# Pooled attention and channel mixing on one core: whole-head preparation and position mixing by a difference

## The chip, the cores and the metric

One NeuronCore of a Trainium2 chip runs the whole program. The metric is the device time of one execution in microseconds, the median over runs. PE, DVE, ACT, POOL and SP are the core's engines: TensorE (matrix products), VectorE, ScalarE, GpSimd and SyncE, the queue that issues the DMAs here.

## What is computed

q, k and v have 8 batches, 8 heads, 1152 positions and 64 channels. Queries are averaged in pairs (576 rows), attention runs over 1152 keys, and the result, with the heads side by side (512 channels), goes through a gated channel mixing:

```python
q_pool = q.reshape(B, H, S // 2, 2, D).mean(axis=3)
scores = scale * np.matmul(q_pool, k.transpose(0, 1, 3, 2))
attn = np.exp(scores - np.max(scores, axis=-1, keepdims=True))
attn = attn / (np.sum(attn, axis=-1, keepdims=True) + 1e-09)
x = np.matmul(attn, v)                        # then heads side by side: (8, 576, 512)
x_prev = np.concatenate([zeros, x[:, :-1, :]], axis=1)
xk = mu_k * x + (1.0 - mu_k) * x_prev
xr = mu_r * x + (1.0 - mu_r) * x_prev
kk = np.maximum(xk @ w_k, 0.0)                # w_k 512 x 1024
vv = kk * kk @ w_v                            # w_v 1024 x 512
out = vv / (1.0 + np.exp(-(xr @ w_r)))        # w_r 512 x 512
```

## The kernel before, in words

**Precision.** Every factor of a product is a pair of 16-bit numbers, a high half and the low half that is left, and a product is the sum of three (high-high, high-low, low-high). So each prepared operand takes a rounding to its high half (ACT), a subtraction that gives the low half (POOL or DVE), and both are stored.

**Attention.** The 64 heads (`n`) of 576 pooled queries are cut into 6 blocks of 96 queries (`NB`, `QN`): 384 blocks. `block` makes the scores of a block into one of three PSUM tiles `s` in two passes of nine products (L528 with the high half of Q, L533 with the low half). Between them DVE takes the maximum over the nine key chunks (L550), PE turns it with the identity (L553), DVE takes the small maximum (L561), and ACT writes it as a row into the Q operand (L542), so that the second pass subtracts it. ACT then takes the exponential (L575) and POOL splits off its low part (L537). `window` sums P x V into the PSUM tile `a` in five windows per head (L602, L604, L607: 18 sums for the first, 27 for each other), DVE divides (L628), and two heads together are turned, from the second batch on with two transposing DMAs, into `xt`, where channels are partitions and positions columns.

**Heads ahead.** `prep` makes K and V of a head: two loads; ACT's rounding of K (L468); the low half of K on POOL (L473, on DVE for head 0); a transposing DMA and a copy; ACT's scaled rounding of V (L492); V's low half on DVE (L495); V for the low products on POOL (L498). `queries` does two heads' Q: load, pair sum (L423, DVE), rounding (L426, ACT), low half (L430, DVE), two transposing DMAs. Both work in two parts, chunks 0 to 4 and 5 to 8.

**Weights.** `weights` brings w_k (8 pieces), w_r (4) and w_v (8): a load, two ACT conversions (L687, L691), a merge on DVE (L694), ACT's rounding (L704), the low half on POOL (L709). The first 8 pieces go by the tiles `ex`, the others by one tile `lw`.

**Channel mixing.** `ff` works on tiles of 256 positions, 18 in all. `mix` makes `xk` and `xr` by channel group (4 groups of 128): ACT scales the earlier position by 1 - mu into a tile `tmp` (L741), DVE multiplies the position by mu and adds (L744). For `xk` ACT rounds (L750); for both POOL takes the low half (L752). A tile then has 96 key products of 256 columns (`wk`), 24 gate products (`wr`) and 48 value products (`wv`) of 512 columns, all at L772. The positions of a tile may lie in two batches; then the steps are split (192 and 64, or 128 and 128).

**Order of issue.** Each step is recorded with `op(engine, duration, function, reads, writes, key)`. `Issue.run` does not sort by key: for each engine it takes the steps in an order that is stored as a compressed table of numbers, `TURNS`. The engines run their queues in that order and wait for one another only by data. `gaps` puts spare matmuls on zeros (L902) into PE's planned pauses of the first 150 us.

The key products of the last batch's tiles may use the PSUM tiles of the scores too (`f_psum`).

## Time and profile before

| | us |
|---|---|
| median of 3 runs | 1087.14 (1086.99 to 1087.65) |
| the profiled execution | 1090.2 |
| its span, first to last instruction | 1088.4 |
| PE busy | 1064.6 (98%) |
| DVE busy | 847.8 (78%) |
| ACT busy | 840.6 (77%) |
| POOL busy | 806.3 (74%) |

Busy time is the time in which at least one instruction of an engine is under way, so one that starts before its neighbour has ended adds only its rest. A matmul is under way from its issue to the end of its result. L numbers are lines of the kernel before; an instruction is named out<-in by the program's tiles.

### The profile page before, as it was taken

Reading aid. Unit: us, or ns where it says so; the run is one execution under the profiler, and the core shown is the slowest. Engines: PE = TensorE matmul, PEld = TensorE weight load, DVE = VectorE, ACT = ScalarE, POOL = GpSimd, SP = SyncE. Lnnn points to the kernel's source line nnn. Section 1 sums busy time; section 2 is a strip of 40 time slices with the busy share of each in tenths; the row PEclk is TensorE's granted clock in tenths of the full one; section 3 lists DMA queues with packets and bytes.
Section 4 is the critical chain, followed back from the end, with each engine's and each line's share of the span. In section 5 each row is a group of like instructions: output and inputs, shape, how many; then the busy total and the mean of one; then the engine's idle time right before and its main releaser. Section 6 shows DMA issues by size and latency. Waiting matters only on the chain.

```text
span 1088.4 us, 43891 instructions
## 1 busy us (share of the span) xinstructions
PE 1064.6 (98%) x18599; PEld 872.8 (80%) x18599; DVE 847.8 (78%) x1590; ACT 840.6 (77%) x1804; POOL 806.3 (74%) x940
## 2 busy tenths in 40 slices
PE   8899999999999999999999999999999999999998
PEld 7888877879698888888697979788787979787664
DVE  7999989888778888788677878787878887774321
ACT  7999987887778887787877788788778778775643
POOL 5889887876787876886777877778677877776431
PEclk9999999999999999999999999999999999999999
DMA  9997838665667664583646646666455565430001
GB/s 229 249 218 182 177 106 187 142 135 111 132 133 145 133 126 112 107 158 85 147 105 127 134 95 143 128 113 147 90 129 125 105 158 116 87 58 20 20 20 39
DMA packets 258148, 135.29 MB, mean 124 GB/s; under 512 B 193440, under 2 KB 230304, under 8 KB 257952
## 3 DMA queue, kind: packets, MB, share of 16 engines
q1 hardware_dynamic: 257952, 132.50, 56.6%
q8 instruction: 145, 2.38, 0.9%
q14 instruction: 51, 0.42, 0.1%
HBM read 67.11 MB, written 9.44 MB: 70 GB/s over the span
## 4 chain that ended last, share of the span: by engine, by line
PE 81%; DVE 5%; issue 1%; ACT 1%; DMA 0%; POOL 0%; SPq 0%; DVEq 0%; ACTq 0%; POOLq 0%
PE f L772 34%; PE s L528 11%; PE s L533 11%; PE a L602 7%; PE a L604 6%; PE a L607 5%; PE s L772 5%; PE s L553 2%; PE a L772 2%; DVE mx L550 2%; DVE vt L495 1%; DVE xr L744 0%; DMA vr<-in_v_dram 0%; DVE mx L561 0%; DVE xk L744 0%
## 5 line engine op out<-in xcount | busy, mean ns | idle before, releaser
L550 DVE TENSOR_REDUCE mx<-s 128x96 f16<-128x864 f32 x384 | 402.6, 1052 | 61.0 <-PE s L528 36.4
L537 POOL TENSOR_SCALAR pl<-pf 128x864 f16<-128x864 uint16 (+1 forms) x384 | 335.0, 872 | 132.6 <-ACT pf L575 106.4
L575 ACT ACTIVATE pf<-s 128x864 int32<-128x864 f32 x384 | 339.4, 887 | 103.3 <-PE s L533 82.6
L602 PE MATMUL a<-vt,pf 128*128 128x65 f16 x2880 | 309.3, 193 | 1.8 <-DVE xb L628 0.7
L604 PE MATMUL a<-vt,pf 128*128 128x64 f16 x2880 | 309.7, 193 | 0.0
L604 PEld LDWEIGHTS <-pf 128*128 128x128 f16 x2880 | 251.4, 98 | 19.0 <-issue 2.5
L602 PEld LDWEIGHTS <-pf 128*128 128x128 f16 x2880 | 256.9, 98 | 11.2 <-issue 0.6
L607 PE MATMUL a<-vb,pl 128*128 128x65 f16 x2304 | 257.7, 193 | 0.7 <-POOL pl L537 0.7
L528 PE MATMUL s<-qT,ks 128*128 128x96 f16 x3456 | 224.8, 206 | 4.2 <-ACT pf L575 2.7
L533 PE MATMUL s<-qT,ks 128*128 128x96 f16 x3456 | 223.8, 206 | 3.6 <-ACT qT L542 1.8
L607 PEld LDWEIGHTS <-pl 128*128 128x128 f16 x2304 | 212.6, 97 | 1.1 <-POOL pl L537 0.9
L528 PEld LDWEIGHTS <-ks 128*128 128x128 f16 x3456 | 186.1, 98 | 31.1 <-issue 5.4
L533 PEld LDWEIGHTS <-ks 128*128 128x128 f16 x3456 | 181.5, 98 | 21.9 <-issue 3.5
L561 DVE TENSOR_REDUCE mx<-s 128x1 f16<-128x128 f32 x324 | 93.3, 288 | 73.3 <-ACT qT L542 70.8
L772 PE MATMUL f<-xhk,wk_hi 128*128 128x256 f16 x496 | 135.2, 273 | 0.8 <-DVE em L836 0.6
L772 PE MATMUL f<-xlk,wk_hi 128*128 128x256 f16 x496 | 135.1, 272 | 0.4 <-POOL xlk L752 0.4
L772 PE MATMUL f<-xhk,wk_lo 128*128 128x256 f16 x496 | 135.2, 273 | 0.0
L542 ACT ACTIVATE qT<-s 1x96 f16<-1x96 f32 x384 | 90.0, 234 | 50.2 <-PE s L553 37.2
L772 PEld LDWEIGHTS <-wk_hi 128*128 128x128 f16 x1152 | 104.7, 98 | 16.3 <-issue 1.0
L473 POOL TENSOR_TENSOR kn<-kr,kn 128x256 f16<-128x256 f32 (+1 forms) x126 | 98.2, 784 | 17.7 <-ACT kn L468 11.0
L803 POOL TENSOR_TENSOR gl<-g 128x512 f16<-128x512 f32 x72 | 76.6, 1066 | 46.4 <-ACT g L801 43.8
L772 PE MATMUL f<-wv_hi,gl 128*128 128x512 f16 x240 | 91.0, 379 | 0.0
(120 smaller groups left out, 2046.2 us busy)
## 6 DMA issues: line engine op xcount, KB each, us to landing
kr<-in_k_dram SPq DMA_DIRECT2D x64, 288.0 KB, 3.7
vr<-in_v_dram SPq DMA_DIRECT2D x64, 288.0 KB, 3.3
qr<-in_q_dram SPq DMA_DIRECT2D x32, 320.0 KB, 3.9
ks<-ks SPq DMA_DIRECT2D x64, 144.0 KB, 3.3
out_dram<-em SPq DMA_DIRECT2D x36, 256.0 KB, 2.7
qr<-in_q_dram SPq DMA_DIRECT2D x32, 256.0 KB, 3.6
xt<-in_moe_w_v_dram SPq DMA_DIRECT2D x8, 512.0 KB, 4.0
st<-in_moe_w_k_dram SPq DMA_DIRECT2D x4, 512.0 KB, 6.1
```

Source lines behind the costliest of these rows:

```text
L473: lambda cs=cs, en=nc.vector if ve else nc.gpsimd: en.tensor_tensor(kn[i][:, cs, D:P], kr[i][:, cs], kn[i][:, cs, 0:D], op=ALU.subtract),
L528: nc.tensor.matmul(cols(c, c + 1), ks1[hp][:, c, :], qhi, start=(c == c0), stop=False, skip_group_check=True)
L533: nc.tensor.matmul(cols(c, c + 1), ks2[hp][:, c, :], qlo, start=False, stop=True, skip_group_check=True)
L537: op("POOL", 0.917 if buf == ("pside",) else NC * (r1 - r0) / 1200 + 0.27, lambda: nc.gpsimd.tensor_scalar(to, half(pf, U16, 0)[:, :, HALF ...
L542: op("ACT", 0.131, lambda: nc.scalar.activation(qlo[0:1], src, AF.Prelu, scale=scale, alpha=(1.0 + EPS) / (1.0 - EPS)), r=[("s", at)] + kl ...
L550: op("DVE", 0.974, lambda: nc.vector.tensor_reduce(mxz[:, P - QN:P], grid(0, NC).rearrange("p c q -> p q c"), axis=AX.X, op=ALU.max), r=[( ...
L561: op("DVE", 0.199, lambda: nc.vector.tensor_reduce(to, s[:, 0:P], axis=AX.X, op=ALU.max), r=[("s", z), ("row", z)], w=[("col", z1) if join ...
L575: op("ACT", NC * QN / 1200 + 0.067, lambda: nc.scalar.activation(pf[:, :, HALF + rows.start:HALF + rows.stop], grid(0, NC), AF.Exp, bias=S ...
L602: nc.tensor.matmul(a_b[:, a0:a0 + VN], half(pf, F16, 1)[:, c, his], vt[jv][:, c, D:D + VN], start=(w == 0 and c == 0), stop=False, skip_gr ...
L604: nc.tensor.matmul(a_b[:, a0:a0 + D], half(pf, F16, 1)[:, c, his], vt[jv][:, c, 0:D], start=False, stop=(side and c == NC - 1), skip_group ...
L607: nc.tensor.matmul(a_b[:, a0:a0 + VN], pl[:, c, rows], vb[jv][:, c, 0:VN], start=False, stop=(c == NC - 1), skip_group_check=True)
L772: nc.tensor.matmul(ps, terms[i][0], terms[i][1], start=(first and i == 0), stop=(i == last), skip_group_check=True)
```

## The change

Four things change, and the order of issue with them.

- `prep` and `queries` work on a whole head (or pair of heads) in one step from the second on; only the first keeps its two parts. The low half of K is DVE's for heads 0 to 7 (`KLO = 8`), POOL's after.
- The low half of the first 12 weight pieces (w_k and w_r) is DVE's (`WLO = 12`), and `lw` has two buffers.
- Mixing takes one difference x - x_prev per pair of channel groups (on DVE, written into the tile of `xr`), and each blend is one multiply-add of the difference with the earlier position. ACT's scaled copies and `tmp` go. The rounding of `xk` is one step per pair, its low half one step per pair on DVE; the low half of `xr` is one step per pair on POOL. The three small scalings of mu go.
- The table `TURNS` is another one (not shown).

```diff
 EARLY = 8
 JOIN = 60
+KLO, WLO = 8, 12
...
-    lw = const.tile([P, 512], F32, name="lw")
+    lw = bufs("lw", 2, [P, 512], F32)
...
         JS = ((0, 5), (5, NQ))
-        for j0, j1 in JS:
+        for j0, j1 in JS if n == 0 else ((0, NQ),):
...
-        for c0, c1 in ((0, 5), (5, NC)):
+        parts = ((0, 5), (5, NC)) if n == 0 else ((0, NC),)
+        for c0, c1 in parts:
...
-            ve = n == 0
+            ve = n < KLO
...
-                if mode == "W3":
+                if iss.nw <= WLO:
+                    op("DVE", 0.6, lambda lo=lo, e=e, hi=hi: nc.vector.tensor_tensor(lo, e, hi, op=ALU.subtract),
+                       r=[ke, ("w", n, c, f)], w=[("wl", n, c, f)], key=key, port=True)
+                elif mode == "W3":
...
-    def mix(w, t0, t1, key, dk):
...
-                op("ACT", ln / 1200 + 0.187, lambda x=x, s0=s0, ln=ln, z=z, c=c: nc.scalar.activation(
-                    tmp[z][:, 0:ln], x[:, c, s0:s0 + ln], AF.Copy, scale=o[:, c:c + 1]),
-   r=xk + [("omu", w)], w=[("tmp", z)], key=key + c * dk)
-                op("DVE", ln / 960 + 0.13, lambda x=x, s0=s0, ln=ln, o0=o0, z=z, c=c: nc.vector.scalar_tensor_tensor(
-                    xm[w][:, c, o0:o0 + ln], x[:, c, s0 + 1:s0 + 1 + ln], m[:, c:c + 1], tmp[z][:, 0:ln],
-                    op0=ALU.mult, op1=ALU.add),
-                   r=xk + [("tmp", z)], w=[("x", w, c, t > t0)], key=key + c * dk, port=True)
...
+    def blend(w, t0, t1, c, key):
+
+        for x, s0, ln, o0, g_, xk in parts(t0, t1):
+            op("DVE", ln / 960 + 0.13, lambda x=x, s0=s0, ln=ln, o0=o0: nc.vector.scalar_tensor_tensor(
+                xm[w][:, c, o0:o0 + ln], xm["r"][:, c, o0:o0 + ln], mu[w][:, c:c + 1], x[:, c, s0:s0 + ln],
+                op0=ALU.mult, op1=ALU.add),
+               r=xk(c) + [("mu", w), ("x", "r", c, g_)], w=[("x", w, c, g_)], key=key, port=True)
+
+    def mix_k(t0, t1, key, dk):
+        n = t1 - t0
+        for c0, c1 in PAIRS:
+            cs = slice(c0, c1)
+            for x, s0, ln, o0, g_, xk in parts(t0, t1):
+                op("DVE", 2 * ln / 960 + 0.069, lambda x=x, s0=s0, ln=ln, o0=o0, cs=cs: nc.vector.tensor_tensor(
+                    xm["r"][:, cs, o0:o0 + ln], x[:, cs, s0 + 1:s0 + 1 + ln], x[:, cs, s0:s0 + ln], op=ALU.subtract),
+                   r=xk(c0) + xk(c0 + 1), w=[("x", "r", c, g_) for c in range(c0, c1)], key=key, port=True)
+            for c in range(c0, c1):
+                blend("k", t0, t1, c, key)
+            op("ACT", 2 * n / 1200 + 0.083, lambda cs=cs: nc.scalar.activation(
+                xh[:, cs, 0:n], xm["k"][:, cs, 0:n], AF.Copy, scale=SK),
+               r=both("k", c0, c1), w=[("xh", c0)], key=key)
+            op("DVE", 2 * n / 960 + 0.069, lambda cs=cs: nc.vector.scalar_tensor_tensor(
+                xl["k"][:, cs, 0:n], xm["k"][:, cs, 0:n], SK, xh[:, cs, 0:n], op0=ALU.mult, op1=ALU.subtract),
+               r=both("k", c0, c1) + [("xh", c0)], w=[("xl", "k", c0)], key=key, port=True)
+            key += 2 * dk
+
+    def mix_r(t0, t1, key, dk):
+        n = t1 - t0
+        hi = top(xm["r"])
+        for c0, c1 in PAIRS:
+            cs = slice(c0, c1)
+            for c in range(c0, c1):
+                blend("r", t0, t1, c, key)
+            op("POOL", 2 * n * 0.0019 + 0.2, lambda cs=cs: nc.gpsimd.tensor_tensor(
+                xl["r"][:, cs, 0:n], xm["r"][:, cs, 0:n], hi[:, cs, 0:n], op=ALU.subtract),
+               r=both("r", c0, c1), w=[("xl", "r", c0)], key=key)
+            key += 2 * dk
```

The lines of the changed kernel are others: its large maximum is L534, the small one L545, the merge of weights L678, their low half L690, a blend L733, the difference L743, the low half of xk L751, and the projections L784.

**DVE in the first heads.** mx and mb are the outputs of the large and the small maximum of a block, ex the merge of a weight piece, vt the low half of V. Before, DVE's queue reads here:

```order
L550 TENSOR_REDUCE mx_98<-s_134 128x96
L561 TENSOR_REDUCE mb_100<-s_133 128x1
L694 SCALAR_TENSOR_TENSOR ex_120<-f,xt_107 128x512
L561 TENSOR_REDUCE mb_101<-s_134 128x1
L495 SCALAR_TENSOR_TENSOR vt_89<-vr_75,vt_89 128x4x64
L694 SCALAR_TENSOR_TENSOR ex_119<-f,st_123 128x512
L495 SCALAR_TENSOR_TENSOR vt_89<-vr_75,vt_89 128x5x64
L550 TENSOR_REDUCE mx_96<-s_132 128x96
```

With the change, at the same head:

```order
L534 TENSOR_REDUCE mx_98<-s_133 128x96
L545 TENSOR_REDUCE mb_100<-s_132 128x1
L690 TENSOR_TENSOR wk_lo<-ex_117,wk_hi 128x512
L545 TENSOR_REDUCE mb_101<-s_133 128x1
L678 SCALAR_TENSOR_TENSOR ex_118<-f,xt_107 128x512
L479 SCALAR_TENSOR_TENSOR vt_89<-vr_75,vt_89 128x9x64
L534 TENSOR_REDUCE mx_96<-s_131 128x96
```

The two halves of V have become one step, and a low half of a weight piece (wk_lo), formerly POOL's, stands between two small maxima.

**DVE where a tile is mixed, in the middle of the program.** Before (xk and xr are blends that read ACT's tmp):

```order
L744 SCALAR_TENSOR_TENSOR xk<-xt_107,mu_k,tmp_118 128x256
L744 SCALAR_TENSOR_TENSOR xk<-xt_107,mu_k,tmp_117 128x256
L827 SCALAR_TENSOR_TENSOR ex_120<-ex_120,em_122 128x512
L836 SCALAR_TENSOR_TENSOR em_122<-f,ex_120 128x512
L550 TENSOR_REDUCE mx_97<-s_133 128x96
```

With the change:

```order
L743 TENSOR_TENSOR xr<-xt_107 128x512
L733 SCALAR_TENSOR_TENSOR xk<-xr,mu_k,xt_107 128x256 x2
L545 TENSOR_REDUCE mx_97<-s_131 128x1
L411 TENSOR_TENSOR qs_78<-qr_77 128x576
L534 TENSOR_REDUCE mx_97<-s_132 128x96
L743 TENSOR_TENSOR xr<-xt_107 128x512
L751 SCALAR_TENSOR_TENSOR xlk<-xk,xhk 128x512
L545 TENSOR_REDUCE mx_98<-s_132 128x1
```

The difference (xr<-xt) comes first, both blends of the pair read it, and the low half of xk (xlk) is DVE's now.

**PE behind the last sum of attention.** wr products belong to the gate of tile 14, wk products to tile 15, wv products to the values of tile 14. Before, the key products stand ahead of the second half of the gate:

```order
L772 LDWEIGHTS wk_lo
L772 MATMUL s_134<-xhk,wk_lo 128x256
L772 LDWEIGHTS wk_hi
L772 MATMUL s_134<-xhk,wk_hi 128x256
L772 LDWEIGHTS xr
L772 MATMUL f<-wr_hi,xr 128x512
L772 LDWEIGHTS xr
L772 MATMUL f<-wr_lo,xr 128x512
```

With the change the gate's twelve products come first, then seventeen value products, and only then the first key product of tile 15:

```order
L784 MATMUL f<-wr_lo,xr 128x512
L784 LDWEIGHTS xlr
L784 MATMUL f<-wr_hi,xlr 128x512
L784 LDWEIGHTS g_113
L784 MATMUL f<-wv_hi,g_113 128x512
L784 LDWEIGHTS g_113
L784 MATMUL f<-wv_lo,g_113 128x512
```

On SP's queue the 31 later Q loads are one transfer each in place of two. PE has 26 more spare matmuls (146 for 120), all before the first products of a tile or shortly after them.

## Rows read from the trace of the kernel before

**Rows 1.** The page's first part: busy us (share of the span) and instructions.

```profile
PE 1064.6 (98%) x18599; PEld 872.8 (80%) x18599; DVE 847.8 (78%) x1590; ACT 840.6 (77%) x1804; POOL 806.3 (74%) x940
```

**Rows 2.** The chain of waits: start us, us, what (pieces of dense stretches).

```profile
165.53 1.51 PE f L772 x7
...
424.98 0.03 PE a L604
...
425.13 0.06 PE s L553
425.19 0.38 PE s L528 x9
...
426.44 0.66 PE f L772 x6
```

**Rows 3.** Busy time by stretch: start:end, its length, busy us of each engine.

```profile
10.00:105.00 95.00, 86.31 (x1940) 77.74 (x1937) 88.73 (x172) 88.10 (x189) 80.00 (x92) 1.00 0.96 221
105.00:193.00 88.00, 84.46 (x1542) 70.77 (x1539) 82.10 (x138) 76.77 (x167) 74.06 (x80) 1.00 0.69 155
193.00:980.00 787.00, 781.93 (x14194) 650.44 (x14191) 638.30 (x1194) 616.74 (x1328) 606.37 (x709) 1.00 0.58 121
980.00:1083.00 103.00, 103.00 (x849) 66.28 (x847) 30.24 (x59) 53.54 (x112) 42.39 (x51) 1.00 0.07 21
```

**Rows 4.** Groups on PE from 193 to 980 us; last, L772 alone in that stretch.

```profile
L604 PE MATMUL a<-vt,pf 128*128 128x64 f16 x2250 | 243.8, 193 | 0.0
...
L607 PE MATMUL a<-vb,pl 128*128 128x65 f16 x1800 | 202.4, 193 | 0.4 <-POOL pl L537 0.4
L528 PE MATMUL s<-qT,ks 128*128 128x96 f16 x2701 | 177.0, 206 | 0.4 <-ACT pf L575 0.3
...
L553 PE MATMUL s<-identb,mx 128*128 128x128 f16 x301 | 66.2, 220 | 2.4 <-DVE mx L550 2.2
...
193.00:980.00 787.00, 444.41 (x2192) 185.76 (x2192) 1.00 0.58 121
```

**Rows 5.** Groups from 10 to 105 us: xcount | busy us, mean ns | idle before.

```profile
L473 POOL TENSOR_TENSOR kn<-kr,kn 128x320 f16<-128x320 f32 x9 | 7.9, 882 | 0.6 <-ACT kn L468 0.2
...
L473 POOL TENSOR_TENSOR kn<-kr,kn 128x256 f16<-128x256 f32 x8 | 5.4, 680 | 0.5
...
L709 POOL TENSOR_TENSOR wk_lo<-ex,wk_hi 128x512 f16<-128x512 f32 x7 | 8.2, 1170 | 2.4 <-PE s L565 1.9
...
L694 DVE SCALAR_TENSOR_TENSOR lw<-lw,xt 128x512 int32<-128x512 int32 x5 | 4.0, 796 | 0.0
...
L495 DVE SCALAR_TENSOR_TENSOR vt<-vr,vt 128x320 f16<-128x320 f32 x7 | 3.6, 510 | 0.0
...
L495 DVE SCALAR_TENSOR_TENSOR vt<-vr,vt 128x256 f16<-128x256 f32 x7 | 3.2, 453 | 0.0
...
L694 DVE SCALAR_TENSOR_TENSOR ex<-f,xt 128x512 int32<-128x512 int32 x4 | 2.7, 679 | 0.0
```

**Rows 6.** Groups of the whole program: the mixing's blend, low half and scaled copies.

```profile
L744 DVE SCALAR_TENSOR_TENSOR xk<-xt,mu_k,tmp 128x256 f32<-128x256 f32 (+3 forms) x96 | 54.2, 571 | 12.0 <-ACT tmp L741 11.5 <-ACT qT L542 0.5
...
L752 POOL TENSOR_TENSOR xlk<-xk,xhk 128x256 f16<-128x256 f32 x72 | 50.7, 711 | 14.4 <-ACT xhk L750 12.0
...
L741 ACT ACTIVATE tmp<-xt,omu_r 128x256 f32<-128x256 f32 (+3 forms) x96 | 42.4, 445 | 9.8 <-DVE xr L744 6.1 <-DVE xk L744 3.5
```

**Rows 7.** DVE in order of time: start us, us, instruction.

```profile
975.72 1.06 DVE L550 TENSOR_REDUCE mx<-s 128x96 f16<-128x864 f32 x1
976.69 0.73 DVE L744 SCALAR_TENSOR_TENSOR xk<-xt,mu_k,tmp 128x64 f32<-128x64 f32 x2
```

**Rows 8.** Groups from 105 to 193 us: the late merges of weights.

```profile
L694 DVE SCALAR_TENSOR_TENSOR lw<-lw,xt 128x512 int32<-128x512 int32 x7 | 6.9, 988 | 0.0
```

**Rows 9.** Waits from 193 to 980 us: us in total, times, longest us.

```profile
DVE mx L561 <- ACT qT L542: 67.1, 113, 1.6
...
PE s L553 <- DVE mx L550: 2.2, 5, 0.7
```

More of the change, by code (lines that the diff above doesn't have):

```diff
@@ L594, in window @@
         VN = D + 1
-        vk = [(x, jv, c0) for x in ("vt", "vtl") for c0 in (0, 5)]
+        vk = [(x, jv, c0) for x in ("vt", "vtl") for c0 in ((0,) if n else (0, 5))]
         js = range(r0 // QN, (r0 + size - 1) // QN + 1)
@@ L683, in v_ @@
                     op("DVE", dur, fn, r=r, w=w, key=key, port=late)
-                u, kf = (lw, ("lw",)) if late else (f_b, ("f",))
+                u, kf = (lw[i], ("lw", i)) if late else (f_b, ("f",))
                 ui = u.bitcast(I32)
@@ L714 @@
     out_f = out.rearrange("b t m -> (b t) m")
-    cnt = {"r32": 0, "ex": 0, "f": 0, "tmp": 0}
+    cnt = {"r32": 0, "ex": 0, "f": 0}
     def turn(n, m=2):
@@ L743, in mix @@
[L743 to L754 removed]
+    PAIRS = [(c, c + 2) for c in range(0, NG, 2)]
@@ new lines, in parts, with both @@
+    def parts(t0, t1):
+        t = t0
+        while t < t1:
+            b = t // TQ
+            e = min(t1, (b + 1) * TQ)
+            s0, ln = t - b * TQ, e - t
+            yield xt[b % 3], s0, ln, t - t0, t > t0, lambda c, b=b, s0=s0, ln=ln: [
+                ("xt", b % 3, c, k0) for k0, k1 in TURN if spans(k0, k1)[0] < s0 + ln and spans(k0, k1)[1] > s0 - 1]
+            t = e
+    def both(w, c0, c1):
+        return [("x", w, c, g_) for c in range(c0, c1) for g_ in (False, True)]
+    def blend(w, t0, t1, c, key):
[4 more added lines that the diff above has]
+               r=xk(c) + [("mu", w), ("x", "r", c, g_)], w=[("x", w, c, g_)], key=key, port=True)
```

215 lines of the change are left out of this document (89 added, 126 removed).

## Prediction

> **What bounds the kernel now.** I first read the page's busy line [rows 1]: PE is busy 1064.6 of 1088.4 us, the other three engines 74 to 78%. That says "TensorE", but a matmul counts as busy while it waits in the pipe, so the second look is at PE's pace. In the chain of waits of a dense stretch nine score matmuls take 0.38 us, six 256-column products 0.66 us, one sum 0.03 us, one identity turn 0.06 us; seven 512-column products take 1.51 us [rows 2]. That is 0.042, 0.11, 0.03, 0.06 and 0.216 us each.
>
> [...] From 193 to 980 us PE issues 6300 sums (two of 2250 and one of 1800), twice 2701 scores, 301 turns and 2192 projection products [rows 4]. A tile has 96 products of 256 columns and 72 of 512, a mean of (96 x 0.11 + 72 x 0.216) / 168 = 0.155 us. So 189 + 228 + 18 + 341 = 776 us of work in 787 us: only some **11 us** are free there. From 980 to 1083 us PE is never idle. The start is different. From 10 to 105 us there are 48 blocks and hardly a projection: 48 x 18 scores x 0.042, at most 8 heads of 126 sums (18 + 4 x 27 in the code) x 0.03 and 48 turns make at most 70 us of work in 95. Here PE waits, and DVE (88.7 us), ACT (88.1) and POOL (80.0) are all nearly full [rows 3]. The stretch from 105 to 193 us is between: DVE 82.1 of 88.
>
> So a gain has two places: about 25 us of PE's free time in the first 105 us, where three engines are full at once, and about 11 us spread over the long middle.
>
> **First stretch (10 to 105 us).** DVE's order up to the 48th row maximum tells what comes and goes. In come seven low halves of K, each 576 columns, and eight low halves of weights of 512. DVE does not show the first at that size. Two halves of V cost 0.510 + 0.453 = 0.963 us; the slope between them (57 ns for 64 columns) gives 0.74 for a whole head [rows 5]. These are the ends; I take 0.75, since the slope comes from the same operation. The weights cost 0.68 as the merge of the same size does [rows 5]. With one difference and one low half of xk (0.68 each, by the same row) that is 7 x 0.75 + 8 x 0.68 + 1.4 = 12.1 us. Out go five late merges (x 0.80 = 4.0), which come later, two blends (1.1 [rows 6]) and fifteen second halves of Q and V, each worth 0.963 - 0.75 = 0.2 (3.0; at the other end nothing). The sum is **+4 us on DVE**, +7 if joining halves saves nothing.
>
> POOL loses seventeen half steps of K (7.9 + 5.4 us) against three whole ones, which cost 0.882 + 0.680 = 1.6 at most, eleven low halves of weights at 1.17 and two of xk at 0.71: 13.3 - 4.7 + 12.9 + 1.4 = **23 us less of 80** [rows 5, 6]. ACT loses four weight chains of three instructions, each at least the 0.445 us of a 256-column step [rows 6], hence 5 us or more, and a fixed part per joined step.
>
> What is late next is therefore DVE. Its 88.7 + 4 would leave 2 of 95 us, but its busy time counts tails that overlap: a row maximum of 1.06 us is followed by the next start after 0.97 [rows 7]. With up to 0.09 us for each of 172 instructions there is room, up to 15 us, which no row settles. With ACT and POOL out of the way I expect DVE to wait less: **-2 us**, between -8 (it closes most gaps) and +4 (every added us lands).
>
> **105 to 193 us.** DVE gets the five late merges (0.99 each in this stretch [rows 8]), four more low weights (2.7), three differences and three low halves of xk (4.1), and loses three blends (1.7), eleven second halves (2.2) and a query step (0.8): +7 on 82.1 of 88. POOL loses 3, ACT the scaled copies of the mixing. PE's own work is some 81 us, so there is little to win. I take **0**, from -3 to +5.
>
> **The middle.** Over the whole program ACT loses 192 scaled copies (2 x 42 us) and POOL 72 low halves of xk (50.7) [rows 6]. DVE keeps the 192 blends and gains a difference and a low half per pair: 48 + 36 operations of up to 0.68 us, at most 57 us. Joining halves gives back 125 x 0.2 = 25. DVE waits 67.1 us for ACT's row write before its small maximum; PE waits for the large maximum, 2.2 us, more than for anything else [rows 9]. A freer ACT shortens the first, a fuller DVE lengthens the second. As 11 us are the most there is to win, I take **-3**, from -8 to +3.
>
> The Q loads lose their halves (31 fewer transfers on SP's queue); they are issued twelve blocks ahead, so I cost the later landing at nothing, and if that cover went, the first score of every second head would wait. The 26 extra filler matmuls stand in planned pauses: 26 x 0.06 = 1.6 us of PE time, nothing unless a pause is gone.
>
> **The end.** The difference is written into the tile of xr, so no tile's key mixing can start before the products of the tile before have read xr. That is a new wait. PE's order now puts the second half of tile 14's gate products ahead of the first key product of tile 15. Behind the last read of the first column pair stand six gate and seventeen value products, 23 x 0.216 = 5.0 us. The chain to cover is a difference (0.68), two blends (2 x 0.57), a copy of 512 columns (under 0.68) and a low half (0.68): 3.2 us and four hand-overs [rows 5, 6]. I cost it at **0**, at most 2 us for each of the last three tiles if DVE is held up.
>
> **Sum.** -2 + 0 - 3 + 0 = -5 us on the profiled execution, whose own time is 1090.2 us (a span of 1088.4 and 1.8 around it). That lies 3.1 us above the median of the runs shown, 1087.14; taken off the median, it gives **1082 us**.
>
> **The rivals.**
> *DVE becomes the bound (slower).* The place is 10 to 193 us. DVE is busy 170.8 of 183 us there, and 4 + 7 are added: 181.8. If its free time cannot be pressed below the 12 us that it has now, the stretch grows by what is added, less what POOL's smaller share lets go: +7, or **1094 us**. It decides as soon as the gaps before the row maxima stay as they are. For it: merges of one size cost 0.68 at one place, 0.80 and 0.99 at others [rows 5, 8], so DVE's work swells where POOL also reads. Against it: POOL is 23 us lighter in just this stretch.
> *xr as a turnstile (slower).* If the chain above takes 7 us in place of 5, PE stands 2 us at each of the last three tiles, where it now has no pause [rows 3]: **1093 us**.
> *Hidden anyway.* DVE's load cancels what ACT and POOL give, and PE's order has the same work: 1087 us.
> *POOL was the true bound of the start.* DVE's two-input steps and POOL's steps hold one another up: the same merge at 0.68, 0.80 and 0.99 us. If they exclude one another, POOL's 80.0 us, DVE's V steps (7 x 0.963 = 6.7), late merges (4.0) and Q steps fill the 95 us, and 23 less on POOL against 8 more on DVE open it until DVE's work ends last: -9 there, -4 in the middle, **1074 us**. [...]
> That the change doesn't do what it says is no rival: the order shows each step where the text puts it.
>
> **How the numbers follow.** A measurement can tell 0.2% (2.2 us) from no change: under 1085.0 is faster, over 1089.3 slower. Chances: the forecast (1077 to 1085) 0.40; POOL as the bound (1068 to 1077) 0.14; hidden 0.18; DVE as the bound (1090 to 1099) 0.20; the turnstile (1090 to 1095) 0.08. So faster 0.54, same 0.18, slower 0.28. The range 1071 to 1095 leaves out the lower part of the POOL case and the upper part of the DVE case, some 0.14. As both signs carry weight, the likeliest case's own range is 1077 to 1085.
>
> **What would show it.** Right: the 48th row maximum starts at 103 us or sooner, DVE busy there at about 92 of 93 us, POOL under 60; PE's free time in the middle under 11 us; no PE wait for xlk after the last sum. Wrong: the 48th block later than 105 us with DVE at its full share, or gaps on PE ahead of the key products of tiles 15 to 17.

## The result, and the profile after

| | before | after |
|---|---|---|
| median of 4 runs, same chip | 1087.39 us | 1103.59 us (1100.48 to 1105.45) |
| ratio, 95% interval | 1 | 1.0139 [1.0108, 1.0170] |
| span of the profiled execution | 1088.4 us | 1098.7 us |

The change is slower by 1.4%; the forecast was 0.5% faster. The profiled execution of after is the fastest of its four, and that of before (1090.2 us) is slower than three of the four beside it, so the two spans lie only 10.3 us apart where the medians lie 16.2 apart: the traces account for 10.3 us. Run again as a control, the changed kernel gives 1.0130 and a span of 1100.6. The page's busy line of after, against [rows 1]:

```profile
PE 1068.2 (97%) x18625; PEld 875.1 (80%) x18625; DVE 873.6 (80%) x1565; ACT 763.0 (69%) x1419; POOL 746.4 (68%) x750
```

ACT lost 78 us and POOL 60, DVE gained 26 and PE 3.6; no other engine is near full, yet the span grew by 10.3. Where it grew is read from the start of the same large maximum in both traces (the blocks numbered from 0). Block 48 starts 3.8 us later than before (108.9 for 105.1), block 80 4.6, the last block 9.6, and the end comes 10.3 later: **3.8 us in the first stretch, 0.8 in the second, 5.0 in the middle, 0.7 at the end**. In the control it is 5.2, 0.2, 6.0 and 0.7. The same stretches of after by windows, to be held against [rows 3] (start:end, length, busy us of PE, weight loads, DVE, ACT and POOL, granted clock, DMA share, GB/s):

```profile
10.00:109.00 99.00, 88.41 (x1957) 80.01 (x1955) 92.47 (x168) 81.11 (x156) 59.56 (x64) 0.98 0.93 199
109.00:198.00 89.00, 85.11 (x1524) 70.57 (x1521) 82.67 (x136) 74.49 (x143) 70.11 (x64) 1.00 0.66 158
198.00:990.00 792.00, 784.11 (x14220) 652.17 (x14218) 653.49 (x1160) 558.73 (x1034) 580.54 (x582) 1.00 0.59 122
990.00:1094.00 104.00, 102.37 (x842) 65.10 (x840) 36.62 (x75) 42.17 (x76) 32.82 (x31) 1.00 0.10 21
```

In the first row POOL fell from 80.0 to 59.6 and ACT from 88.1 to 81.1, DVE rose from 88.7 to 92.5: each as forecast. But the stretch is 4 us longer, and the granted clock is 0.98 where it was 1.00. The windows inside show where, first before, then after:

```profile
20.00:24.00 4.00, 2.84 (x68) 2.54 (x66) 3.47 (x5) 3.61 (x7) 3.41 (x5) 1.00 1.36 254
24.00:28.00 4.00, 3.85 (x98) 3.69 (x99) 2.99 (x7) 3.26 (x9) 2.00 (x4) 1.00 0.83 279
28.00:32.00 4.00, 3.62 (x89) 3.29 (x85) 3.87 (x10) 4.00 (x7) 3.67 (x5) 1.00 1.20 242
```

```profile
20.00:24.00 4.00, 3.99 (x114) 3.86 (x110) 3.63 (x6) 3.84 (x7) 3.41 (x4) 1.00 0.97 311
24.00:28.00 4.00, 1.29 (x24) 1.30 (x25) 1.71 (x4) 0.99 (x2) 0.17 (x1) 0.81 1.20 157
28.00:32.00 4.00, 3.48 (x58) 3.25 (x56) 2.46 (x4) 2.88 (x6) 0.00 (x0) 0.76 1.14 177
```

From 20 to 24 us PE issues 114 matmuls where it issued 68; then it stands for most of four microseconds and the others do little, and the clock is 0.81 and 0.76 over these windows (0.50 from 26.5 to 29.9 us). PE and its weight loads by time in after (start, us, instruction, in brackets the idle time before it and what ended it):

```profile
23.76 0.19 PE L588 MATMUL a<-vt,pf 128*128 128x64 f16 x1
23.79 0.20 PE L591 MATMUL a<-vb,pl 128*128 128x65 f16 x1
...
26.70 0.10 PEld L586 LDWEIGHTS <-pf 128*128 128x128 f16 x1 [2.84 <-issue]
26.71 0.24 PE L586 MATMUL a<-vt,pf 128*128 128x65 f16 x1 [2.72 <-issue]
26.76 0.25 PE L588 MATMUL a<-vt,pf 128*128 128x64 f16 x1
26.81 0.25 PE L591 MATMUL a<-vb,pl 128*128 128x65 f16 x1
```

PE stops for 2.7 us in the middle of a window of sums whose operands are all there: "issue" means that no semaphore ended the pause. Behind it the sums stand 0.05 us apart instead of 0.03, at this clock of 0.50. Before has one such pause, of 0.6 us at 73.4 us.

The waits of the middle (195 to 1000 us: who waits for whom, us in total, times, longest), against [rows 9]:

```profile
PE s L537 <- DVE mx L534: 3.8, 10, 1.0
PE s L537 <- DVE mx L545: 1.8, 4, 0.7
```

Before, PE waited 2.2 us for the maxima; now 5.6 for both: 3.4 us more, of the middle's 5.0. So three places are to be explained: a stop without a wait, waits for DVE in the middle, and 0.7 us at the end.

### The profile page after: what moved, and what is told of

The parts are those of the page before. It is cut to its first block, busy times and chain, and to the rows that moved or that the text cites. A ratio compares the mean times of both kernels' runs of the same rounds, so it can differ in the third digit from the quotient of the medians.

```text
span 1098.7 us, 43186 instructions
## 1 busy us (share of the span) xinstructions
PE 1068.2 (97%) x18625; PEld 875.1 (80%) x18625; DVE 873.6 (80%) x1565; ACT 763.0 (69%) x1419; POOL 746.4 (68%) x750
## 3 DMA queue, kind: packets, MB, share of 16 engines
q1 hardware_dynamic: 257456, 132.49, 57.3%
q8 instruction: 145, 2.38, 0.9%
## 5 line engine op out<-in xcount | busy, mean ns | idle before, releaser
L521 POOL TENSOR_SCALAR pl<-pf 128x864 f16<-128x864 uint16 (+1 forms) x384 | 353.7, 921 | 190.5 <-ACT pf L559 157.9
L534 DVE TENSOR_REDUCE mx<-s 128x96 f16<-128x864 f32 x384 | 402.4, 1052 | 57.1 <-PE s L512 39.8
L586 PE MATMUL a<-vt,pf 128*128 128x65 f16 x2880 | 302.0, 193 | 4.2 <-issue 2.7
L588 PE MATMUL a<-vt,pf 128*128 128x64 f16 x2880 | 302.3, 193 | 0.0
L591 PE MATMUL a<-vb,pl 128*128 128x65 f16 x2304 | 254.2, 193 | 0.0
L545 DVE TENSOR_REDUCE mx<-s 128x1 f16<-128x128 f32 x324 | 92.9, 287 | 66.0 <-ACT qT L526 64.0
L784 PE MATMUL f<-xhk,wk_hi 128*128 128x256 f16 x496 | 135.1, 272 | 0.9 <-DVE em L848 0.7
L784 PE MATMUL f<-xlk,wk_hi 128*128 128x256 f16 x496 | 135.1, 272 | 0.2 <-DVE xlk L751 0.2
L784 PE MATMUL f<-xhk,wk_lo 128*128 128x256 f16 x496 | 135.2, 273 | 0.0
L784 PEld LDWEIGHTS <-wk_hi 128*128 128x128 f16 x1152 | 105.8, 98 | 15.1 <-issue 1.3
L815 POOL TENSOR_TENSOR gl<-g 128x512 f16<-128x512 f32 x72 | 79.0, 1104 | 39.7 <-ACT g L813 25.9
L537 PE MATMUL s<-identb,mx 128*128 128x128 f16 x384 | 84.5, 221 | 8.9 <-DVE mx L534 5.6
L784 PE MATMUL f<-wv_hi,g 128*128 128x512 f16 x240 | 90.9, 379 | 1.2 <-ACT ex L832 1.2
```

Of the source, the lines that this page charges most:

```text
L521: op("POOL", 0.917 if buf == ("pside",) else NC * (r1 - r0) / 1200 + 0.27, lambda: nc.gpsimd.tensor_scalar(to, half(pf, U16, 0)[:, :, HALF ...
L534: op("DVE", 0.974, lambda: nc.vector.tensor_reduce(mxz[:, P - QN:P], grid(0, NC).rearrange("p c q -> p q c"), axis=AX.X, op=ALU.max), r=[( ...
L537: op("PE", 0.057, lambda: nc.tensor.matmul(s[:, 0:P], mxz, identb, start=False, stop=False, skip_group_check=True), r=[("mx", z), ("col", ...
L545: op("DVE", 0.199, lambda: nc.vector.tensor_reduce(to, s[:, 0:P], axis=AX.X, op=ALU.max), r=[("s", z), ("row", z)], w=[("col", z1) if join ...
L586: nc.tensor.matmul(a_b[:, a0:a0 + VN], half(pf, F16, 1)[:, c, his], vt[jv][:, c, D:D + VN], start=(w == 0 and c == 0), stop=False, skip_gr ...
L588: nc.tensor.matmul(a_b[:, a0:a0 + D], half(pf, F16, 1)[:, c, his], vt[jv][:, c, 0:D], start=False, stop=(side and c == NC - 1), skip_group ...
```

## The experiments

The middle's waits are given below as in that view, the two rows of the maxima added. The expectations also count them otherwise: by how much later than the median distance PE reaches the identity turns (about 5 us before, 10 after and 11 in the control, with delays under 0.12 us left out). All ratios are to the kernel before on the same chip; stops and waits are those of one profiled execution each.

| kernel | ratio [95%] | block 48 later by | PE's stops without a wait, to 80 us | waits for maxima |
|---|---|---|---|---|
| control: after again | 1.0130 [1.0113, 1.0147] | 5.2 | 3.7 | 6.3 |
| e1 a load later | 1.0152 [1.0127, 1.0176] | 4.1 | 3.1 | 5.3 |
| e8 fillers in halves | 1.0110 [1.0090, 1.0130] | 3.2 | 2.7 | 7.3 |
| e2 difference in its own tile | 1.0135 [1.0120, 1.0150] | 3.8 | 3.7 | 6.3 |
| e3 low half of xk on POOL | 1.0242 [1.0221, 1.0263] | 5.5 | 4.6 | 8.9 |
| e14 without low half of xk | 1.0123 [1.0103, 1.0144] | 8.0 | 4.4 | 6.9 |
| e17 and without difference | 1.0104 [1.0089, 1.0118] | 4.1 | 4.7 | 6.3 |
| e15 without the second V | 1.0130 [1.0111, 1.0149] | 3.8 | 3.0 | 6.5 |
| e5 after, table 1 | 1.0077 [1.0059, 1.0095] | 5.3 | 3.9 | 2.9 |
| e9 after, table 2 | 1.0103 [1.0080, 1.0126] | 4.9 | 2.8 | 3.7 |
| e6 before, table 1 | 1.0061 [1.0041, 1.0081] | 6.3 | 0.7 | 4.5 |
| e13 before, table 2 | 0.9979 [0.9968, 0.9990] | 1.1 | 0.9 | 1.0 |
| e7 whole heads, table 1 | 1.0021 [1.0010, 1.0033] | 2.3 | 0.5 | 2.0 |
| e10 whole heads, table 2 | 1.0032 [1.0020, 1.0044] | 3.3 | 2.0 | 0.7 |
| e11 mixing, table 2 | 1.0103 [1.0087, 1.0119] | 4.6 | 4.0 | 2.3 |
| e12 both, low halves on POOL, table 2 | 1.0041 [1.0021, 1.0060] | 6.1 | 4.6 | 2.6 |
| e18 e12, fillers in halves | 1.0041 [1.0026, 1.0056] | 1.4 | 1.4 | 2.8 |
| e19 e9, fillers in halves | 1.0042 [1.0029, 1.0056] | 2.7 | 0.4 | 3.0 |

### The stop at 24 us

The control is the changed kernel with no edit.

> The changed kernel once more, nothing edited, so that its parts can be told beside the edits on the same chip. In its first trace PE stands from 23.99 to 26.71 us in the middle of a group of nine sums, at matmuls that wait for no engine, the granted clock is 0.76 to 0.81 from 24 to 32 us, and the 16th row maximum starts 4.3 us later than before. If that is a cause that belongs to the kernel, the pause is there again, 2 to 3 us at 24 us. If it was an accident of one execution, it is gone here and the time is some 4 us less than in the other runs. Either way the end should show 2.1 us of PE's waiting for xlk and the key mixing near 1010 and 1019 us, and the middle PE's waits for the large maximum of some 10 us in all.

It repeats the loss. A first guess at the stop was that PE's code, whose transfers the page counts on the same 16 DMA engines as the loads (0.9% of their span, the loads' queue 57.3%), was late behind three loads of weights in a row. e1 issues the third behind the transposition for Q (the spare matmuls, which follow from the plan, become five fewer with it):

```diff
 SP: st<-w_k, ks, xt<-w_k
-xt<-w_k
 qT<-qn (transposition)
+xt<-w_k
```

> The third load of weights is issued behind the transposition of Q for head 2, as in the kernel before, and no longer straight behind the second load; nothing else is moved on any queue. Theory A (the pause at 24 us is PE out of code: its next piece came at 24.37 us, when the three loads of 512 KB issued between 16.4 and 18.6 us had landed): the piece comes before 22 us, the pause of 2.7 us and the low clock are gone, the 16th row maximum starts at 41.5 us and not at 45.6, and the time falls by 4 us, to a ratio of 1.010 to the kernel before. Theory B (the order of PE, DVE and ACT around head 2 makes the pause, the loads have no part in it): pause, clock and time stay, ratio 1.014. Middle and end do not change under either.

The load did move, as SP's queue shows, from 17.58 (two loads there) to 24.37 us (start, us, transfer; after, then e1):

```profile
16.39 0.57 SPq L663 DMA_DIRECT2D st<-in_moe_w_k_dram  x1
17.05 0.47 SPq L471 DMA_DIRECT2D ks<-ks  x1
17.58 1.05 SPq L663 DMA_DIRECT2D xt<-in_moe_w_k_dram  x2
23.01 1.70 SPq L434 DMA_TRANSPOSE qT<-qn  x1
```

```profile
17.54 0.58 SPq L666 DMA_DIRECT2D xt<-in_moe_w_k_dram  x1
22.49 1.82 SPq L437 DMA_TRANSPOSE qT<-qn  x1
24.37 0.91 SPq L666 DMA_DIRECT2D xt<-in_moe_w_k_dram  x1
...
26.22 0.23 PE L589 MATMUL a<-vt,pf 128*128 128x65 f16 x1 [2.22 <-issue]
```

The stop stayed, 2.2 us: the guess was too narrow. But the same trace, with the others, shows what the stop is. Number PE's instructions from 0 in their order (matmuls, weight loads and the few semaphore instructions between them). The stops over 0.25 us before 80 us then stand at 705, 1217, 1729, 2241 and 2753, once at 1473 (e10), in the kernels with split fillers (below) at 961, 1985 and 2497, and one later at 22465 (e9): always 449 + a multiple of 256, in every kernel, and before's own single one is 2753. A transfer of PE's instruction queue has 16,384 bytes (2.38 MB in 145, the page's row of the DMA queue), and after's 37,316 instructions of PE are 145.8 times 256:

```profile
q8 instruction: 145, 2.38, 0.9%
```

In after the second of these transfers starts at 24.37 us and PE goes on at 26.71; in the control 24.18 and 26.60, in e1 23.80 and 26.22: 2.3 to 2.4 us later each time. In all the traces there are 43 such stops up to 105 us, and each ends 1.2 to 1.7 us after the end of the transfer of its piece; no border was crossed sooner than 2.2 us after the start of its transfer. So PE had used up its code. A piece's transfer starts near PE's crossing of the border before it (from 0.7 us ahead of it to 5.8 us behind it, median 1.9), so PE has little more than one piece of code ahead. In after PE was ready for the second piece some 4.8 us behind the border at 449 (before it got there in 6.8), and the transfer started 5.2 us behind that border (before 3.1, at 21.47 us): PE was quicker and the piece was later. Either alone would have stopped it for less than 1 us, by an estimate from these times and the 2.3 us. The view of the DMA queues has the piece in 24 to 26 us in after (a packet's whole time counts where it starts, so a share can pass 100%):

```profile
q1 hardware_dynamic: 529, 0.18, 146.6%
q8 instruction: 1, 0.02, 3.4%
```

If that is so, other boundaries between pieces must move the stop although no step moves. e8 splits the fillers that go to the tile `a` into two matmuls of 64 columns: the same columns, 166 instructions more.

```diff
-        for _ in range(k):
-            nc.tensor.matmul(to, zero, zero, ...)
+        h = P // 2 if z is None else P
+        for _ in range(k * P // h):
+            nc.tensor.matmul(to[:, 0:h], zero, zero[:, 0:h], ...)
```

> The changed kernel, in which each filler matmul of 128 columns into the tile of the sums (some 60 of them up to 16 us, ahead of the first scores above all) is two of 64 columns: the same columns, but some 120 more instructions on PE early on. Where a piece of PE's code ends moves by that many instructions ahead in the work. Theory A (PE runs out of code at 24 us because the piece asked for at about 18 us waits behind bulk loads): the piece is asked for before 16 us, ahead of the weights' loads, and lands before it is needed; the pause of 2.1 to 2.7 us at 24 us and the low clock after it are gone, the 16th row maximum starts at 43 us or sooner and not at 45.6, and the time falls by 2 to 4 us, ratio 1.010. Theory B (order around head 2): the pause stays where the same sums stand, ratio 1.013.

```profile
20.00:24.00 4.00, 3.75 (x107) 3.64 (x104) 3.63 (x5) 3.71 (x7) 3.41 (x4) 1.00 0.98 308
24.00:28.00 4.00, 3.22 (x80) 2.92 (x77) 3.99 (x8) 2.96 (x6) 0.13 (x1) 1.00 1.24 229
```

The border at 449 comes at 15.62 us, ahead of the loads, and the second piece starts 1.1 us behind it, at 16.70 us. PE issues nearly as densely as in after and does not stop at 24 us; the clock stays at 1.00, and block 16 starts 1.4 us later than before, not 4.3. Later pieces still stop it for 0.8, 0.3 and 1.6 us, and the ratio went only from 1.0130 to 1.0110, with overlapping intervals. The clear case is e19, the same edit on e9 (below), where all but 0.4 us of the stops went:

> All steps of the changed kernel, the second search's table (1.0103; 2.8 us of pauses for code up to 55 us, one of 1.1 us at 622 us), and the same split of the fillers. Theory A: pauses up to 80 us under 1 us in all, ratio 1.006 to 1.008. Beside the kernel above it tells what the moved low halves cost or give in the first 105 us once the code is out of the way: if DVE is the bound there, its 48th row maximum starts 2 us or more later than that kernel's; if not, within 1 us.

1.0103 became **1.0042**, with intervals apart. Moving the borders is worth some 0.6% there. Of this the profiles show 3.5 us, 0.3%, as stops that are gone: 2.4 us up to 80 us, and one of 1.1 us at 622 us that e9 has and e19 has not. The rest is not shown; two of e9's six executions lie some 5 us or more above its others.

### The end

e2 gives the difference a tile of its own (`lw`, free by then) from tile 4 on, so that key mixing need not wait for the products that read xr.

```diff
-                xm[w][:, c, o0:o0 + ln], xm["r"][:, c, o0:o0 + ln], mu[w][:, c:c + 1], ...
+                xm[w][:, c, o0:o0 + ln], lw[c // 2].rearrange("p (c t) -> p c t", c=2)[:, c % 2, o0:o0 + ln], mu[w][:, c:c + 1], ...
```

> From the fifth tile on the difference of neighbouring rows is written into a tile of its own (the weights' scratch, free by then) and not into the tile of xr, so the key mixing of a tile no longer waits until the gate products of the tile before have read xr. No order is touched. Theory C (the turnstile costs what PE waits at the end): PE's pauses at 1010.75 us (1.34 us) and 1019.3 us (0.62 us) and the like shrink to less than 0.3 us, and the time falls by 2 us, ratio 1.012. Theory D (the pauses come from DVE being late there whatever the tile): they stay, ratio 1.014. In the middle, up to 1 us less if the turnstile holds up DVE's queue there as well, which its busy share of 0.83 speaks against.

1.0135, and the waits of 990 to 1092 us are the same, in after and in e2:

```profile
PE f L784 <- ACT ex L832: 1.2, 1, 1.2
PE s L784 <- DVE xlk L751: 0.5, 1, 0.5
```

```profile
PE f L801 <- ACT ex L849: 1.2, 1, 1.2
PE s L801 <- DVE xlk L768: 0.5, 1, 0.5
```

So xr as a turnstile costs nothing in this order. PE stands between the gate and the value products of tile 14's second half, 1.2 us, until ACT has read the gate from the PSUM tile `f`. The timeline of after:

```profile
1009.20 0.38 PE L784 MATMUL f<-wr_hi,xlr 128*128 128x512 f16 x1
1010.75 0.38 PE L784 MATMUL f<-wv_hi,g 128*128 128x512 f16 x1 [1.17 <-ACT ex L832]
```

In the order before, key products stand among the gate products there, as the section on the change shows. Another order at this place was not tried alone. That this pause makes the 0.7 us is not shown: e8, e14, e17 and e9 have the same pause of 1.2 us, and their ends come 0.0 us later or, in e9, 0.2 us sooner. The kernels that are alike at the end (after, the control, e1, e8, e15) spread from 0.0 to 0.9 us.

### The middle: too much work on DVE or POOL?

e3 takes the low half of xk back to POOL (for all tiles but those of the last batch; a scale of 1 lets POOL subtract).

```diff
-SK = 2.0 ** -4
+SK = 1.0
-            op("DVE", ..., lambda cs=cs: nc.vector.scalar_tensor_tensor(
-                xl["k"][:, cs, 0:n], xm["k"][:, cs, 0:n], SK, xh[:, cs, 0:n], op0=ALU.mult, op1=ALU.subtract),
+            op("DVE" if tail else "POOL", ..., lambda cs=cs, en=nc.vector if tail else nc.gpsimd: en.tensor_tensor(
+                xl["k"][:, cs, 0:n], xm["k"][:, cs, 0:n], xh[:, cs, 0:n], op=ALU.subtract),
```

> The low half of xk is made on POOL again, a column pair at a time, for all tiles but those of the last batch entry; that takes some 30 steps of 0.68 us and more off DVE, 20 us of its 715 in the middle, and puts 30 of about 1.2 us on POOL. So that POOL can do it with one subtraction, x is not scaled by 1/16 ahead of the split (and the products are not scaled back). Theory E (in the middle PE waits for the large maximum because DVE is too full): PE's waits for it fall from 10 to about 6 us between 195 and 1000 us, time 4 us less, ratio 1.010. Theory F (DVE is held up by long steps that stand ahead of a maximum and swell beside POOL's, whoever makes xlk): one kind of long step less, but more steps on POOL to collide with; waits stay within 1 us, ratio 1.013 to 1.015. If the later xlk is what counts, PE waits for it ahead of the key products instead, and the ratio rises over 1.015.

It is 1% worse than after, and PE now waits for POOL's low half as well. Its waits:

```profile
PE s L540 <- DVE mx L537: 6.4, 13, 1.0
PE f L788 <- POOL xlk L755: 2.8, 4, 1.6
PE s L540 <- DVE mx L548: 2.5, 5, 0.9
```

That says that the step fits DVE better in this order, not that DVE is innocent. So e14, e17 and e15 leave steps out and keep after's order: the low half of xk from tile 4 on; the difference too; the copy of V for the low products from head 8 on (POOL).

```diff
-... lambda cs=cs: nc.vector.scalar_tensor_tensor(xl["k"]...
+... lambda cs=cs: t0 < 4 * T and nc.vector.scalar_tensor_tensor(xl["k"]...
...
-... lambda x=x, ...: nc.vector.tensor_tensor(xm["r"][:, cs, o0:o0 + ln], ...
+... lambda x=x, ...: t0 < 4 * T and nc.vector.tensor_tensor(xm["r"][:, cs, o0:o0 + ln], ...
...
-        op("POOL", 0.75, lambda: nc.gpsimd.tensor_scalar(
+        op("POOL", 0.75, lambda: n < H and nc.gpsimd.tensor_scalar(
```

> The changed kernel with its own order; from the fifth tile on the low half of xk is not made (the products read what an earlier tile left there). That takes some 28 steps of 0.68 us and more off DVE in the middle, 20 of its 715 us, and nothing else. Theory J (DVE's added steps between the maxima make PE wait there): PE's waits ahead of the identity turns between 195 and 1000 us fall from 10.8 to some 7.5 us, the time by 3 us, ratio 1.010. Theory K (it is not their number; a DVE step that meets one of POOL's waits it out, and that hits whatever stands there): no more than 1 us, ratio 1.012 to 1.014.

> As the one beside it, and the difference is not made either from the fifth tile on (the blend takes the neighbouring row in its place): some 28 and 36 steps less, 45 of DVE's 715 us in the middle, so that DVE has less to do than in the kernel before. Theory J: the waits ahead of the identity turns fall to the 5 us of the kernel before or under it, the time by 6 us against the changed kernel, ratio 1.007; what is left is the start. Theory K: at most 2 us, ratio 1.011 or more.

> The changed kernel with its own order; from the second batch entry on POOL does not make the scaled copy of V (the sums read an earlier head's). That takes 56 steps of 0.67 us off POOL, 33 of its 593 us in the middle, and nothing off DVE. Theory K (PE waits because DVE's two-input steps and POOL's steps hold each other up): DVE's long ones (blends and differences of 1.2 to 1.7 us where 0.5 to 0.8 is usual) get fewer by more than a tenth, the waits ahead of the identity turns fall by 2 us or more, ratio 1.011 or less. Theory J: no change within 1 us, ratio 1.013.

The same window in the kernel before, the control, e17 and e15:

```profile
195.00:1000.00 805.00, 799.93 (x14461) 663.78 (x14458) 646.40 (x1212) 627.88 (x1350) 619.06 (x722) 1.00 0.57 119
```

```profile
195.00:1000.00 805.00, 796.07 (x14467) 662.45 (x14466) 662.11 (x1173) 565.95 (x1049) 591.71 (x591) 1.00 0.59 121
```

```profile
195.00:1000.00 805.00, 797.12 (x14477) 663.26 (x14476) 631.40 (x1123) 566.96 (x1051) 585.47 (x592) 1.00 0.60 121
```

```profile
195.00:1000.00 805.00, 795.63 (x14461) 662.11 (x14459) 656.55 (x1173) 565.88 (x1049) 550.80 (x541) 1.00 0.59 121
```

e17's DVE is 15 us lighter than before's and still PE waits for it as long as in the control (control, then e17):

```profile
PE s L537 <- DVE mx L534: 3.5, 9, 1.0
PE s L537 <- DVE mx L545: 2.8, 5, 1.0
```

```profile
PE s L540 <- DVE mx L537: 4.0, 8, 1.0
PE s L540 <- DVE mx L548: 2.3, 4, 1.0
```

With 41 us less on POOL (e15) the time is the control's, 1.0130. The waits of the middle are therefore not a matter of how full DVE or POOL is. What is left is where in its queue each maximum stands: the order. The traces bear this out: nine of e17's twelve waits for a maximum, 4.8 of its 6.3 us, stand at blocks where the control waits too, and eleven of e15's fourteen. The longest of after, 1.0 us at 499.7 us, and the same place in e17 (DVE by time):

```profile
497.07 1.38 DVE L839 SCALAR_TENSOR_TENSOR ex<-ex,em 128x512 f32<-128x512 f32 x1
...
498.58 1.04 DVE L534 TENSOR_REDUCE mx<-s 128x96 f16<-128x864 f32 x1
```

```profile
498.33 1.39 DVE L842 SCALAR_TENSOR_TENSOR ex<-ex,em 128x512 f32<-128x512 f32 x1
```

The step of the gate (`ex`) ahead of the two maxima (the small one, not shown, stands between) takes 1.4 us here; the median of the 26 in the middle is 0.73. In after 3.5 of the 5.6 us of waits stand behind such a DVE step of 1.3 to 1.8 us, next to the maxima in the queue. Why single steps are that long is open: with 41 us less on POOL, 3 of 26 gate steps over 1.2 us became 4.

### The order

For the next kernels the table `TURNS` was searched anew, table 1 for one set of durations, table 2 for the mean over four sets, three of them lengthened at random. The steps are those of after (e5, e9), of before (e6, e13), of before with after's `prep` and `queries` and only the first low half on DVE (e7, e10), of after with before's `prep` and `queries` and low halves of K and the weights on POOL (e11), and of after with these low halves on POOL (e12; e18 with split fillers). The last three have this line:

```diff
-KLO, WLO = 8, 12
+KLO, WLO = 1, 0
```

> Every step of the changed kernel is kept, with its engine, tiles and waits; only the table of turns is another, searched anew by moving single steps of DVE, ACT, PE and POOL along their queues (the order of the DMA issues is kept). Theory G (the loss sits in the order that came with the change: PE, DVE and ACT wait at places where another order of the same steps would not): PE's waits for the maxima between 195 and 1000 us fall from 10 to 5 us or less, the pause of 1.34 us between gate and value products at 1011 us is gone, the time falls by 8 us or more, ratio 1.005 or less. Theory H (the loss sits in the steps: DVE has more to do and longer steps, whatever the order): the waits for the maxima stay at 8 us or more, ratio 1.010 or more. The pause at 24 us, PE out of code, may stay under either and is worth 3 to 4 us.

> All steps of the changed kernel with a table of this second search. Theory G (the order makes the loss): within 0.3% of the kernel before with its table of the same search. Theory H (the steps make it): 0.5% or more above that, with PE's waits for the maxima between 195 and 1000 us well over that kernel's. PE's pauses for code between 24 and 80 us, 3 to 4 us, may be here in any order, as the kernel before has 0.6 us of them: they are counted apart.

With the changed kernel's steps untouched, PE's waits for the maxima fell from 6.3 to 2.9 and 3.7 us, and the time by 0.5% and 0.3% (e9's interval still overlaps the control's). The middle of the traces grew by 1.6 us (e5) and 3.4 (e9) where it grew by 6.0 in the control. e5's ratio lies between what its two theories gave. e9's waits:

```profile
PE s L540 <- DVE mx L537: 2.7, 4, 1.4
PE s L540 <- DVE mx L548: 1.0, 2, 0.9
```

> The kernel before with a table of turns searched anew in the same way; all steps kept. It says what such a search is worth where the steps are the old ones. If theory G holds and the old table was near what the search can find, 0.995 to 1.002. If the search gains as much here as with the changed kernel's steps (ratio 0.990 or less), a lower time of the changed kernel with a new table says nothing on its steps.

> The kernel before with a second table searched anew: this search takes the mean over four sets of durations, three of them with steps, hand-overs and landings made longer at random, so that the order is not fitted to one set. It is the measure for the three beside it, whose tables come from the same search. If such a table carries over to the chip better than the first (ratio 1.006), 0.995 to 1.004; if not, 1.005 or more, and only differences between the four count.

The steps of before, in two tables, lie 0.8% apart: 1.0061 and **0.9979**. The second beats both kernels by a little. Before's steps wait 4.5 us for the maxima under table 1 and 1.0 under table 2; of the second:

```profile
PE s L556 <- DVE mx L553: 1.0, 3, 0.4
```

> The kernel before with one part of the change alone: from the second head on Q's load and sum, the roundings and low halves of Q, K and V are one step each and not two; K's low halves and those of the weights stay on POOL, the mixing is the old one. The table is searched anew as in the two kernels beside it. DVE, ACT and POOL lose the fixed part of some 125, 190 and 63 instructions. Theory G: within 0.3% of the kernel before in its new order, since neither engine sets the middle. Theory H (long steps ahead of a maximum cost): slower than it by 0.5% or more, with PE's waits for the maxima over 8 us.

> The kernel before with whole-head steps alone, table of the second search. If joining halves is free or a gain: 0.996 to 1.001 of the kernel before with its table of this search. If a long step ahead of a maximum costs PE time: 1.003 or more of it.

> The kernel before with the new mixing alone (a difference for each column pair, a multiply-add for each blend, both low halves a pair at a time, that of xk on DVE; the weights' scratch doubled as in the change), heads prepared in halves, low halves of K and of the weights on POOL; table of the second search. Theory H in its form for the mixing (84 more steps of 0.68 us on DVE between the maxima make PE wait): 1.005 or more of the kernel before with its table of this search. Theory G: within 0.3% of it.

> The changed kernel with the low halves of K (heads 1 to 7) and of the first twelve pieces of weights back on POOL, with a table of the second search; to be set beside the changed kernel with its table of that search (1.0103, 48th row maximum 4.9 us later than in the kernel before, 2.8 us of it PE's pauses for code). Theory L (DVE is the bound of the first 105 us, and these steps cost what they take): the 48th row maximum starts 2 us or more sooner, ratio 1.008. If POOL was the bound, as the rival of the prediction had it: 2 us or more later, ratio 1.012 or more. If neither sets it: within 1 us but for the pauses for code.

> The kernel with the low halves of K and of the weights back on POOL and the second search's table (1.0041, in whose trace PE stands 4.7 us for code at 25.6, 53, 68 and 80 us), with each 128-column filler into the tile of the sums as two of 64. Theory A (PE runs out of code): the pieces end 120 instructions sooner in the work, where the time from asking to needing is 7.6 us or more for the pieces up to 60 us; less than 2 us of such pauses, the granted clock 1.00 throughout, the time 3 to 4 us less, ratio 1.000 to 1.001. If pauses of that kind follow the work and not the code's pieces, they stay at 25, 53 and 68 us, ratio 1.004.

Whole heads alone give +0.2 and +0.3%, the mixing alone +1.0% in its one table; yet both together with the low halves on POOL give +0.4%, so 1% is no price of the mixing (4.0 us of stops stand in e11's profile). By what was expected of them, the two tables speak against each other. Under table 2 the changed steps (e9), whole heads (e10) and the mixing (e11) lie 1.2, 0.5 and 1.2% above e13, and e9 waits 3.7 us for the maxima to e13's 1.0, as the theory had it that blames the steps. Under table 1 the changed steps (e5) lie 0.2% above e6 and whole heads (e7) 0.4% below it, which is nearer to the theory that blames the order; e6 is itself slower than was expected of it. So a share of the steps in the middle's loss is neither shown nor excluded.

e12 and e18 have the same ratio with 4.6 and 1.4 us of stops in their profiles; but e18's profile is one of its faster executions, and the stops differ from one execution to the next (2.7 in after, 3.7 in the control). Of three pairs with split fillers only e9 and e19 show a gain that is clear of the intervals.

## Why the prediction was wrong

**The first stretch: forecast -2, measured +3.8 (control +5.2).** The failed step is "With ACT and POOL out of the way I expect DVE to wait less", the one with no row of its own. DVE's work up to block 48 grew by 3.7 us, as costed (+4), but DVE's idle time stayed: 6.3 of 95 us before, 6.5 of 99 after. PE got through its sums earlier, as meant, and outran its code, and DVE stood with it. The sentences "The 26 extra filler matmuls ... nothing unless a pause is gone" and on the Q loads, "I cost the later landing at nothing", priced instructions and transfers only by time on an engine or a wait for data. They also move the borders between code pieces and the transfers beside them: e8 shows that fillers alone do it. Which of the change's parts made the 2.7 us is not shown. Without most of the stops, e19 can be held against the terms (10 us to the start of its block 48):

```profile
10.00:107.80 97.80, 87.64 (x1991) 79.46 (x1989) 93.63 (x168) 81.76 (x157) 60.66 (x66) 1.00 0.93 205
```

DVE +4.9 (forecast +4), ACT -6.3 (5 or more), POOL -19.3 (23): **the engine terms were nearly right.** DVE's idle time fell, to 4.2 us, yet block 48 still starts 2.7 us late, so 19 us less on POOL and 6 on ACT did not make up for what DVE got. e18, with the low halves left on POOL, has +1.4 with 1.0 us more of stops, a hint that the halves moved to DVE cost some 2 us there (2.7 - 0.4 against 1.4 - 1.4). It is no more than a hint: kernels that are all but alike up to block 48 (after, the control, e2, e14, e15, e17) spread from +3.8 to +8.0, and e18 ends no sooner than e19.

**105 to 193 us: forecast 0, measured +0.8** (control +0.2). Right, though DVE's +7 came as no more than 82.7 busy us of 89.

**The middle: forecast -3 (-8 to +3), measured +5.0.** The step that failed is "A freer ACT shortens the first, a fuller DVE lengthens the second": waits were tied to how full an engine is, and the range was drawn from there. The first half won nothing that shows. The second is refuted by e17: with DVE 15 us below before's, the waits stay, at the same places. They depend on the places that the new table gives the maxima, and two other tables take about half of them away; whether the rest belongs to the steps is open. The row to distrust was [rows 9]: with before's own steps the waits are 2.2, 4.5 or 1.0 us by the table, so 2.2 us was the merit of a table that fitted its steps, not spare room.

**The end: forecast 0, measured +0.7.** The chain of the turnstile was priced right at nothing (e2). The one new pause is a read by ACT of a PSUM tile, which the text on the moved gate products did not look at; that it makes the 0.7 us is not shown.

**The rivals.** The turnstile falls with e2. "POOL was the true bound of the start" falls with e19. DVE's blends do swell beside POOL's steps: of before's 96 of 256 columns, the 22 with no POOL step beside them took 0.47 to 0.48 us, the 24 with POOL busy for over nine tenths of their time 0.49 to 1.60, 0.98 on average; POOL's low halves of K of 256 columns took 0.67 us on average with no blend, low half, pair sum or gate step (`ex`) of DVE beside them, 0.81 with one for over 0.2 us. What makes the blends differ so much is open, and the swelling sets no end here: in the middle, 41 us of POOL's work less (e15) leave 1.0130. Of "DVE becomes the bound" there is the hint above, and e17 speaks against it in the middle. "Hidden anyway" falls with the loss. None named the code or the table.

**What stays open.** Another table and moved code borders took the changed steps from 1.0130 to 1.0042 (e19): two thirds of the loss went with no step of the change touched. e19's last 0.42%, 4.6 us, can't be divided between the steps and the table, as two tables of the same steps differ by 0.8%. The middle's loss can't be divided between them either, nor is it known what makes single DVE steps twice as long as their like. Which transfers delay a code piece is not settled either.

## What to carry to other kernels

An order written as a table is fitted to its steps; a change of steps brings its own table, and with two tables of the same steps 0.8% apart, neither result prices the steps. Where a change lets PE run through many small matmuls beside bulk loads, look at where its code pieces end: a stop inside a group whose idle time ends in "issue" is the sign. Waits for an engine don't tell that it is too full: leave work out and see if they go, and look which step stands ahead of what is waited for.

## What was not expected of the hardware

**PE can outrun its code.** Stops of 0.3 to 2.8 us stand at instruction 449 + a multiple of 256, and PE goes on 1.2 to 1.7 us after the end of the transfer of the 16,384-byte piece, in all 43 stops up to 105 us. All 145 transfers of the queue in after have that size. Not every border stops PE: beside that at 705 (2.7 us), after crosses nine up to 75 us, each within 0.04 us from one start to the next. **Behind the longest stop the clock is lower**: the windows show 0.81 and 0.76, where before and e8 (20 to 28 us), which did not stop there, have 1.00. The control, e1 and e15 have it behind this stop too (2.1 to 2.2 us), and their block 16 starts 3.7 to 4.3 us late; e2, e3 and e17, with stops of 1.8 to 2.2 us at the same instruction and a clock of 1.00 there, are 2.6 to 3.4 us late. By this the low clock costs about 1 us, an estimate, and not every long stop brings it.
